# Narrow tiles paired in one PSUM bank, and the stream's steps forwarded by 400 instructions, in an attention with interleaved feed-forward work

## The chip, the cores and the metric

The kernel runs on one core of a Trainium2 chip: TensorE (matmuls, into PSUM), VectorE, ScalarE, GpSimd, and the queue of SyncE, which issues all DMAs here. The metric is the device time of one execution in microseconds. Rows of the profile call the engines PE (PEld: its weight loads), DVE, ACT, POOL and SP.

## What is computed

Three stages in a row, in float32, on B = 2 batches, 8 heads, 768 positions of head dimension 64; after the attention that is 1536 tokens of width 512:

```python
scores = scale * np.matmul(q, k.transpose(0, 1, 3, 2))
keep = is_sink | in_window            # 4 sink columns, window of 128
a = softmax(np.where(keep, scores, -1e9))
x = np.matmul(a, v)                   # -> 1536 x 512
h = x @ w_in                          # 512 -> 2048
x = (h * np.tanh(log1p(exp(h)))) @ w_out     # 2048 -> 512
p = domain_probs / domain_probs.sum(-1)      # 4 experts
out = sum(p[:, e] * (np.maximum(x @ w1[e], 0) @ w2[e]) for e in range(4))   # 512 -> 1024 -> 512
```

## The kernel before

**Attention.** `banded` walks 24 items (batch, block of 256 queries, pair of heads; the pairs run fastest, so that four items in a row finish 256 tokens). An item makes four score tiles on TensorE (L231), a masked copy with row minimum on VectorE (L234), the exponential on ScalarE (L238), a scaling on GpSimd (L252, L255), transposes (L264), and the product with the values, one tile `pv` of matmuls L277 and L283. `evac_x` then copies `pv` into the token matrix as a high part `xh` (ScalarE, L184) and a low part `xl` (VectorE, L185). There is one `pv` buffer, so the next item's `pv` waits for this copy. Items 0 to 23 are counted below; L185 of an item is called its evacuation.

**Feed-forward.** It is cut into units of 512 hidden columns: four units with the smooth activation, then eight of the experts. A product is done as three matmuls of high and low parts (`TERMS`). `stream` takes one chunk of tokens of a unit after the other: `layer1` makes hidden tiles `h` of 128 hidden columns by the chunk's tokens (L477), `mish` turns each into `gh` and `gl` (five ScalarE passes and the copy `gh`, VectorE L553, L555 and L556, GpSimd for `gl`), and `layer2` makes output tiles `o` (L504) and copies them into `acc`. Unit 0 is cut into chunks of 256, 256, 512 and 512 tokens, called c0 to c3. Chunk c0 needs items 0 to 3, c1 items 4 to 7, c2 items 8 to 15, c3 items 16 to 23. Each tile is a step of the generator; layer 1 of a chunk and layer 2 of the one before alternate. The loop over the items takes a step at every item from 5 on.

During the attention `h` and `o` have one PSUM bank each, and `mish` one buffer `r`; a new `h` waits until L556 has read the one before. When the attention's pools close, three banks each and two for `r` take their place (`x.psum(ctx, 3, 3, 2)`), and the weights of unit 1 (`wi1`, `wo1`) are loaded into memory that the attention's pools and that `r` held.

**Weights.** The first two layers' weights come as 64-bit numbers. `split_double` converts a quarter of a matrix at a time by seven VectorE passes over 1024 columns (L117 to L124). Ten such conversions lie within the attention: four for unit 0, six for `wi1`, `wo1` and `wi2`, which are parked in DRAM and loaded later. The eleventh, for `wo` of unit 2, is put out later in the program.

**Order.** The program is handed to a list scheduler. Each instruction has a place in the order in which the code puts it out; by its own timeline the scheduler picks, for each engine, among the instructions that are ready the one with the earliest place. The engines then run their lists in that order, each waiting where its next instruction is not ready. All DMAs stand in SP's one list.

## Time and profile before

| | us |
|---|---|
| runs shown | 929.54, 937.5, 939.44 (median 937.5) |
| the profiled execution, its own time | 931.33 |
| its span, first to last instruction | 929.5 |
| TensorE busy | 905.6 |
| VectorE, ScalarE, GpSimd busy | 424.6, 347.7, 263.7 |

The span holds all but 1.8 us of the profiled time. "Busy" of TensorE joins pipelined matmuls with modelled ends, so it is no measure of how full the engine is. The first 164 us hold the attention, the rest the feed-forward stages.

### The profile page before, as it was taken

To read this page: it belongs to the slowest core of one execution; us is meant where nothing else is said; L and a number is where in the kernel's file an instruction comes from. 1 tells how busy PE (TensorE), PEld (TensorE's weight loads), DVE (VectorE), ACT (ScalarE), POOL (GpSimd) and SP (SyncE) were. 2 spreads that over 40 slices of the span, in tenths; PEclk is the share of its full clock that TensorE was granted. 3 is DMA by queue.
4 is the path that set the end of the run, shared out by engine and by line. 5 is a ranking of instruction groups with operands and counts; after the bars stand their busy time and mean duration, and the time that the engine had idled before them with its cause. 6 is when DMAs were issued, how large, how long until landed. Compare 5 with 4: busy or idle time off the path is not lost.

```text
span 929.5 us, 11138 instructions
## 1 busy us (share of the span) xinstructions
PE 905.6 (97%) x4292; PEld 730.6 (79%) x4292; DVE 424.6 (46%) x770; ACT 347.7 (37%) x745; POOL 263.7 (28%) x217
## 2 busy tenths in 40 slices
PE   6999999799999999999999999999999999999997
PEld 4566767688888888888888888888888888888886
DVE  6999995247698555641112222222222222222222
ACT  4788875487767767722221111111111111111110
POOL 4586663122222434520220220221122112200000
PEclk8999999989999999999999999999999999999999
DMA  7757752062123011001110110110110010000012
GB/s 234 249 189 242 251 215 80 17 255 91 46 90 136 1 46 46 23 23 46 46 40 7 45 46 1 46 46 0 46 46 24 23 45 1 1 1 1 11 46 83
DMA packets 33790, 67.03 MB, mean 72 GB/s; under 512 B 4144, under 2 KB 12592, under 8 KB 33728
## 3 DMA queue, kind: packets, MB, share of 16 engines
q1 hardware_dynamic: 33728, 66.23, 21.1%
q8 instruction: 36, 0.59, 0.3%
q14 instruction: 26, 0.21, 0.1%
HBM read 51.54 MB, written 9.44 MB: 66 GB/s over the span
## 4 chain that ended last, share of the span: by engine, by line
PE 86%; DVE 10%; ACT 1%; DMA 1%; issue 0%; POOL 0%; DVEq 0%; ACTq 0%
PE h L477 42%; PE o L528 28%; PE o L504 14%; DVE pr L234 2%; DVE cv_h L119 1%; DVE cv_a L123 1%; PE pv L277 1%; DVE cv_a L117 1%; DVE cv_r L122 1%; DMA stage<-in_moe_w_in_dram 1%; PE sc L231 1%; PE tp L264 1%; DVE cv_a L121 1%; DVE xl L185 1%; DVE cv_a L118 0%
## 5 line engine op out<-in xcount | busy, mean ns | idle before, releaser
L477 PE MATMUL h<-xh,wih 128*128 128x512 f32 (+1 forms) x592 | 229.2, 387 | 0.3 <-DVE w L556 0.3
L477 PE MATMUL h<-xh,wil 128*128 128x512 f32 (+1 forms) x592 | 227.8, 385 | 0.0
L477 PE MATMUL h<-xl,wih 128*128 128x512 f32 (+1 forms) x592 | 226.8, 385 | 0.0
L486 ACT ACTIVATE gh<-h 128x512 fp32r<-128x512 f32 x96 | 57.4, 598 | 410.1 <-PE h L477 245.2
L487 DVE SCALAR_TENSOR_TENSOR gl<-h,gh 128x512 fp32r<-128x512 f32 x96 | 66.4, 691 | 208.1 <-ACT gh L486 207.9
L528 PE MATMUL o<-wol,gh 128*128 128x512 f32 (+1 forms) x388 | 150.1, 387 | 0.0
L528 PE MATMUL o<-woh,gh 128*128 128x512 f32 (+1 forms) x388 | 150.1, 387 | 0.0
L528 PE MATMUL o<-woh,gl 128*128 128x512 f32 (+1 forms) x388 | 149.9, 387 | 0.0
L536 DVE SCALAR_TENSOR_TENSOR acc<-o,pn,acc 128x512 f32<-128x512 f32 (+1 forms) x85 | 63.3, 745 | 176.2 <-PE o L528 176.2
L477 PEld LDWEIGHTS h<-xh,wih 128*128 128x128 f32 x592 | 111.8, 189 | 24.5 <-DVE cv_a L117 0.7
L477 PEld LDWEIGHTS h<-xl,wih 128*128 128x128 f32 x592 | 111.5, 189 | 22.6 <-issue 0.5
L477 PEld LDWEIGHTS h<-xh,wil 128*128 128x128 f32 x592 | 111.7, 189 | 22.3 <-DVE wil L124 0.3
L97 POOL TENSOR_TENSOR gl<-w,gh 128x512 fp32r<-128x512 f32 (+1 forms) x52 | 68.2, 1312 | 168.0 <-ACT gh L89 167.8
L504 PE MATMUL o<-gh,woh 128*128 128x512 f32 (+1 forms) x208 | 79.4, 382 | 5.4 <-ACT gh L89 5.4
L528 PEld LDWEIGHTS o<-wol,gh 128*128 128x128 f32 x388 | 72.9, 188 | 14.9
L528 PEld LDWEIGHTS o<-woh,gh 128*128 128x128 f32 x388 | 72.9, 188 | 14.9
L528 PEld LDWEIGHTS o<-woh,gl 128*128 128x128 f32 x388 | 72.8, 188 | 14.7
L504 PE MATMUL o<-gh,wol 128*128 128x512 f32 (+1 forms) x208 | 78.2, 376 | 0.0
L504 PE MATMUL o<-gl,woh 128*128 128x512 f32 (+1 forms) x208 | 77.4, 379 | 0.0
L87 POOL TENSOR_SCALAR wih<-stage 128x1024 fp32r<-128x1024 f32 x16 | 16.5, 1048 | 189.4 <-PE h L477 189.4
L553 DVE SCALAR_TENSOR_TENSOR u<-w,r 128x512 f32<-128x512 f32 (+1 forms) x52 | 34.4, 662 | 50.2 <-ACT r L552 49.9
L87 POOL TENSOR_SCALAR woh<-stage 128x1024 fp32r<-128x1024 f32 x16 | 16.5, 1048 | 141.0 <-PE o L528 122.2
(84 smaller groups left out, 1101.5 us busy)
## 6 DMA issues: line engine op xcount, KB each, us to landing
stage<-in_moe_w_dram SPq DMA_DIRECT2D x32, 512.0 KB, 3.7
stage<-in_moe_w_in_dram SPq DMA_DIRECT2D x8, 1024.0 KB, 6.6
stage<-in_moe_w_out_dram SPq DMA_DIRECT2D x8, 1024.0 KB, 5.0
qk<-in_qk_dram SPq DMA_DIRECT2D x16, 324.0 KB, 5.4
acc<-in_v_dram SPq DMA_DIRECT2D x16, 192.0 KB, 3.6
woh<-cv_h SPq DMA_DIRECT2D x6, 512.0 KB, 2.9
out_dram<-acc SPq DMA_DIRECT2D x11, 256.0 KB, 2.0
wih<-cv_h SPq DMA_DIRECT2D x4, 512.0 KB, 3.0
```

What stands on the lines that cost most here:

```text
L87: eng.tensor_scalar(out, src, 1.0, 0.0, ALU.mult, ALU.add)
L97: eng_lo.tensor_tensor(lo, src, hi.bitcast(F32), ALU.subtract)
L117: nc.vector.tensor_scalar(af, af, TINY_HI, HUGE_HI, ALU.max, ALU.min)
L119: nc.vector.scalar_tensor_tensor(h, w_hi, -0x40000000, a, ALU.bitwise_and, ALU.bitwise_or)
L234: nc.vector.tensor_tensor_reduce(out=o, in0=sc, in1=c.masks[t if i == 0 else 2][:, 0:sw], scale=-c.scale, scalar=3.0e38, op0=ALU.add, op1= ...
L477: nc.tensor.matmul(h, lhsT=wis[sw][:, k, fs], rhs=x[sx][:, k, cols], start=k == 0 and t == 0, stop=k == KT - 1 and t == 2,)
L486: nc.scalar.activation(gh, h, AF.Relu)
L487: nc.vector.scalar_tensor_tensor(gl, h, 0.0, gh.bitcast(F32), ALU.max, ALU.subtract)
L504: nc.tensor.matmul(o, lhsT=wos[sw][:, f, ds], rhs=g[f][sx], start=f == 0 and t == 0, stop=f == NF - 1 and t == 2,)
L528: nc.tensor.matmul(o, lhsT=g[f][sx][:, ds], rhs=wos[sw][:, f, ms], start=f == 0 and t == 0, stop=f == NF - 1 and t == 2,)
L536: nc.vector.scalar_tensor_tensor(y, o, pcol, y, ALU.mult, ALU.add)
L553: nc.vector.scalar_tensor_tensor(u, w, 1.0, r, ALU.add, ALU.mult)
```

## The change

`layer1` and `layer2` take as many tiles as fit into a bank of 512 columns: for the chunks of 256 tokens two hidden tiles stand side by side in one `h`, and two output tiles in one `o`, each pair with one set of passes behind it; a step is then a pair. Chunks of 512 are as before. Unit 0's four chunks have 20 steps in place of 28. They are taken at items 5, 7, 9, 11, 13, 15 and 17 to 23 (13 steps, in place of 19 at items 5 to 23), within `tc.high_priority(offset=FORWARD)`: the instructions of such a step get a place in the order that is 400 earlier (an item is some 40 instructions). Item 23's step is now the first `h` of c3, in the attention's bank; before it was an `o` of c1.

```diff
--- before.py
+++ after.py
@@ -26,8 +26,9 @@
 QW = 2 * P
 STAGE = 1024
 AHEAD = 2
-LAG = 5
 WARM = 12
+STEPS = (5, 7, 9, 11, 13, 15, *range(17, 24))
+FORWARD = 400
 PARK = (8, 10, 12, 14, 16, 18)
 
 class Ctx:
@@ -469,23 +470,26 @@
         x = (c.xh, c.xl)
         cols = slice(t0, t0 + cw)
         wis = self.w[n][0]
-        for f in range(NF):
-            h = self.pa.tile([P, self.CW], F32, tag="h", name="h")[:, 0:cw]
-            fs = slice(f * P, (f + 1) * P)
-            for k in range(KT):
-                for t, (sw, sx) in enumerate(TERMS):
-                    nc.tensor.matmul(
-                        h, lhsT=wis[sw][:, k, fs], rhs=x[sx][:, k, cols],
-                        start=k == 0 and t == 0, stop=k == KT - 1 and t == 2,
-                    )
-            gh = self.gp.tile([P, self.CW], F32R, tag="gh", name="gh")[:, 0:cw]
-            gl = self.gp.tile([P, self.CW], F32R, tag="gl", name="gl")[:, 0:cw]
+        m = self.CW // cw
+        parts = [slice(q * cw, (q + 1) * cw) for q in range(m)]
+        for f0 in range(0, NF, m):
+            h = self.pa.tile([P, self.CW], F32, tag="h", name="h")
+            for f, at in enumerate(parts, f0):
+                fs = slice(f * P, (f + 1) * P)
+                for k in range(KT):
+                    for t, (sw, sx) in enumerate(TERMS):
+                        nc.tensor.matmul(
+                            h[:, at], lhsT=wis[sw][:, k, fs], rhs=x[sx][:, k, cols],
+                            start=k == 0 and t == 0, stop=k == KT - 1 and t == 2,
+                        )
+            gh = self.gp.tile([P, self.CW], F32R, tag="gh", name="gh")
+            gl = self.gp.tile([P, self.CW], F32R, tag="gl", name="gl")
             if kind == 0:
                 self.mish(n, gh, gl, h)
             else:
                 nc.scalar.activation(gh, h, AF.Relu)
                 nc.vector.scalar_tensor_tensor(gl, h, 0.0, gh.bitcast(F32), ALU.max, ALU.subtract)
-            g.append((gh, gl))
+            g.extend((gh[:, at], gl[:, at]) for at in parts)
             yield
 
     def layer2(self, n, t0, cw, g):
@@ -496,22 +500,25 @@
         wos = self.w[n][1]
         if kind == 0:
             accv = self.acc.rearrange("p (ch d) w -> p ch d w", d=KT)
-            for d in range(KT):
-                o = self.pb.tile([P, cw], F32, tag="o", name="o")
-                ds = slice(d * P, (d + 1) * P)
-                for f in range(NF):
-                    for t, (sw, sx) in enumerate(TERMS):
-                        nc.tensor.matmul(
-                            o, lhsT=wos[sw][:, f, ds], rhs=g[f][sx],
-                            start=f == 0 and t == 0, stop=f == NF - 1 and t == 2,
-                        )
-                y = accv[:, t0 // c.DM, d, t0 % c.DM:t0 % c.DM + cw]
+            m = self.CW // cw
+            for d0 in range(0, KT, m):
+                o = self.pb.tile([P, self.CW], F32, tag="o", name="o").rearrange("p (m w) -> p m w", m=m)
+                for d in range(d0, d0 + m):
+                    ds = slice(d * P, (d + 1) * P)
+                    for f in range(NF):
+                        for t, (sw, sx) in enumerate(TERMS):
+                            nc.tensor.matmul(
+                                o[:, d - d0], lhsT=wos[sw][:, f, ds], rhs=g[f][sx],
+                                start=f == 0 and t == 0, stop=f == NF - 1 and t == 2,
+                            )
+                ds = slice(d0, d0 + m)
+                y = accv[:, t0 // c.DM, ds, t0 % c.DM:t0 % c.DM + cw]
                 if n == 0:
                     nc.scalar.activation(y, o, AF.Copy)
                 else:
                     nc.vector.tensor_tensor(y, y, o, ALU.add)
                 if n == n1 - 1:
-                    split(c, c.xh[:, d, cols], c.xl[:, d, cols], y, nc.scalar, nc.vector)
+                    split(c, c.xh[:, ds, cols], c.xl[:, ds, cols], y, nc.scalar, nc.vector)
                 yield
             return
         last = n == len(self.units) - 1
@@ -589,15 +596,16 @@
         attention_item(c, a, *it, preps.pop(m))
         if m < 4 or m in PARK:
             run(w, 1)
-        if m >= LAG:
-            run(steps, 1)
+        if m in STEPS:
+            with tc.high_priority(offset=FORWARD):
+                run(steps, 1)
         if m == 0:
             normalize_probs(c)
     first.close()
     x.wpool[1] = ctx.enter_context(tc.tile_pool(name="m_w1", bufs=1))
     x.psum(ctx, 3, 3, 2)
     run(x.weights(1))
-    run(steps, 4 * (x.NF + 4) - 4 - (len(items) - LAG))
+    run(steps, 2 + 4 + 6 + 8 - len(STEPS))
     rest(c, x, steps, 1)
```

Three places show what the scheduler made of it. Names carry buffer numbers; line numbers of the changed kernel are one higher in the attention, L481 for L477 and L510 for L504.

VectorE at the evacuation of item 19 (`pv_1709` before, `pv_1641` now); the rows named `cv` are the eleventh conversion. First the kernel before, then the changed one.

```order
L234 ISA pr_1969,mx_1970<-sc_1980,mask260_90 128x260
L234 ISA mx_1970 128x1
L185 TENSOR_TENSOR xl_95<-pv_1709,xh_94 128x256
L234 ISA pr_1969,mx_1970<-sc_1984,mask260_90 128x260
L234 ISA mx_1970 128x1
L555 SCALAR_TENSOR_TENSOR u_1321<-u_1321,r_1322 128x256
L556 SCALAR_TENSOR_TENSOR w_1320<-u_1321,h_1305 128x256
L117 TENSOR_SCALAR cv_a_2400<-cv_a_2400 128x1024
L118 TENSOR_SCALAR cv_a_2400<-cv_a_2400 128x1024
L240 RECIPROCAL sm_1971<-sm_1971 128x4
L119 SCALAR_TENSOR_TENSOR cv_h_2402<-stage_60,cv_a_2400 128x1024
L185 TENSOR_TENSOR xl_95<-pv_1779,xh_94 128x256
```

```order
L118 TENSOR_SCALAR cv_a_2328<-cv_a_2328 128x1024
L119 TENSOR_SCALAR cv_a_2328<-cv_a_2328 128x1024
L120 SCALAR_TENSOR_TENSOR cv_h_2330<-stage_60,cv_a_2328 128x1024
L241 RECIPROCAL sm_1846<-sm_1846 128x4
L122 TENSOR_SCALAR cv_a_2328<-cv_h_2330 128x1024
L123 TENSOR_SCALAR cv_r_2329<-cv_h_2330 128x1024
L235 ISA pr_1925,mx_1926<-sc_1936,mask260_90 128x260
L235 ISA mx_1926 128x1
L124 SCALAR_TENSOR_TENSOR cv_a_2328<-stage_60,cv_a_2328 128x1024
L235 ISA pr_1925,mx_1926<-sc_1940,mask260_90 128x260
L235 ISA mx_1926 128x1
L186 TENSOR_TENSOR xl_95<-pv_1641,xh_94 128x256
```

Six passes of the eleventh conversion stood behind that evacuation and stand ahead of it now.

TensorE after the last hidden tile that uses the attention's bank: `h_1941`, the fourth of c2, before; `h_1978`, the first of c3, now. `gh_1803` and `gh_1910` belong to the tile before it in that bank, `gh_1954` to `h_1941`, and `gh_1991` to `h_1978`. First before, then changed.

```order
L477 MATMUL h_1941<-xl_95,wih_227 128x512
L504 MATMUL o_2139<-gh_1803,woh_353 128x512
L504 MATMUL o_2139<-gh_1803,wol_354 128x512
L504 MATMUL o_2181<-gh_1803,woh_353 128x512
L504 MATMUL o_2181<-gh_1803,wol_354 128x512
L504 MATMUL o_2223<-gh_1803,woh_353 128x512
L504 MATMUL o_2223<-gh_1803,wol_354 128x512
L504 MATMUL o_2139<-gl_1804,woh_353 128x512
L504 MATMUL o_2181<-gl_1804,woh_353 128x512
L504 MATMUL o_2223<-gl_1804,woh_353 128x512
L504 MATMUL o_2139<-gh_1954,woh_353 128x512
L504 MATMUL o_2139<-gh_1954,wol_354 128x512
```

```order
L481 MATMUL h_1978<-xl_95,wih_227 128x512
L510 MATMUL o_2067<-gh_1910,woh_353 128x512
L510 MATMUL o_2067<-gh_1910,wol_354 128x512
L510 MATMUL o_2067<-gl_1911,woh_353 128x512
L510 MATMUL o_2109<-gh_1910,woh_353 128x512
L510 MATMUL o_2109<-gh_1910,wol_354 128x512
L510 MATMUL o_2109<-gl_1911,woh_353 128x512
L510 MATMUL o_2151<-gl_1483,woh_353 128x512
L510 MATMUL o_2151<-gh_1581,woh_353 128x512
L510 MATMUL o_2151<-gh_1581,wol_354 128x512
L510 MATMUL o_2151<-gl_1582,woh_353 128x512
L510 MATMUL o_2151<-gh_1747,woh_353 128x512
```

Before, nine matmuls stand between the tile and the first use of its `gh`; in the changed kernel 28 do (the list goes on with `o_2151` and `o_2165`, then `o_2239<-gh_1991`).

SP's queue at the end of the attention: `wi1`, `wo1` are unit 1's weights, `wi2` unit 2's first, which overwrites unit 0's. First before, then changed.

```order
L372 DMA stage_60<-in_moe_w_in_dram 128x2x1024
L434 DMA wih_2057<-wi1h_792 128x1024
L434 DMA wil_2058<-wi1l_793 128x1024
L434 DMA wih_2057<-wi1h_792 128x1024
L434 DMA wil_2058<-wi1l_793 128x1024
L434 DMA woh_2063<-wo1h_1137 128x1024
L434 DMA wol_2064<-wo1l_1138 128x1024
L434 DMA woh_2063<-wo1h_1137 128x1024
L434 DMA wol_2064<-wo1l_1138 128x1024
L434 DMA wil_2308<-wi2l_1451 128x1024
L434 DMA wih_2307<-wi2h_1450 128x1024 x2
```

```order
L373 DMA stage_60<-in_moe_w_in_dram 128x2x1024
L435 DMA wil_2236<-wi2l_1397 128x1024
L435 DMA wih_2235<-wi2h_1396 128x1024 x2
L435 DMA wil_2236<-wi2l_1397 128x1024
L435 DMA wih_2027<-wi1h_788 128x1024
L435 DMA wil_2028<-wi1l_789 128x1024
L435 DMA wih_2027<-wi1h_788 128x1024
L435 DMA wil_2028<-wi1l_789 128x1024
L435 DMA woh_2033<-wo1h_1115 128x1024
L435 DMA wol_2034<-wo1l_1116 128x1024
L435 DMA woh_2033<-wo1h_1115 128x1024
```

The four loads of `wi2` stood behind those of `wi1` and `wo1`, and stand ahead of them now.

## Rows read from the trace of the kernel before

**Rows 1.** The page: busy us (share) xcount; 40 slices in tenths; granted clock.

```profile
PE 905.6 (97%) x4292; PEld 730.6 (79%) x4292; DVE 424.6 (46%) x770; ACT 347.7 (37%) x745; POOL 263.7 (28%) x217
...
DVE  6999995247698555641112222222222222222222
...
PEclk8999999989999999999999999999999999999999
```

**Rows 2.** Four stretches: busy us (instructions) of each engine, granted clock, DMA share, GB/s.

```profile
100.00:120.00 20.00, 20.00 (x139) 14.47 (x140) 19.66 (x48) 17.23 (x54) 13.39 (x15) 1.00 0.82 280
120.00:140.00 20.00, 18.66 (x124) 12.62 (x125) 19.97 (x51) 15.72 (x48) 13.30 (x15) 0.91 0.54 193
140.00:160.00 20.00, 20.00 (x133) 16.18 (x130) 10.26 (x13) 11.05 (x28) 6.51 (x7) 1.00 0.23 81
180.00:200.00 20.00, 15.22 (x54) 12.29 (x55) 8.26 (x12) 15.10 (x28) 4.96 (x4) 0.83 0.77 284
```

**Rows 3.** Timeline of VectorE: start us, length us, what ran, [idle before].

```profile
138.20 0.41 DVE L185 TENSOR_TENSOR xl<-pv,xh 128x256 fp32r<-128x256 f32 x1
...
139.84 1.03 DVE L117 TENSOR_SCALAR cv_a<-cv_a 128x1024 f32<-128x1024 f32 x1
...
146.44 1.22 DVE L123 SCALAR_TENSOR_TENSOR cv_a<-stage,cv_a 128x1024 f32<-128x1024 uint32 x1
...
163.86 0.42 DVE L185 TENSOR_TENSOR xl<-pv,xh 128x256 fp32r<-128x256 f32 x1 [0.33 <-ACT xh L184]
```

**Rows 4.** VectorE groups by shape, 20 to 164 us: xcount | busy, mean ns.

```profile
L555 DVE SCALAR_TENSOR_TENSOR u<-u,r 128x256 f32<-128x256 f32 x8 | 3.5, 434 | 0.0
...
L555 DVE SCALAR_TENSOR_TENSOR u<-u,r 128x512 f32<-128x512 f32 x2 | 1.4, 692 | 1.4 <-ACT u L554 1.4
```

**Rows 5.** Timeline of TensorE in the attention.

```profile
128.49 0.38 PE L477 MATMUL h<-xh,wih 128*128 128x256 f32 x1 [0.25 <-DVE w L556]
...
161.68 1.09 PE L277 MATMUL pv<-pt,acc 128*64 128x256 f32 x12
...
163.34 0.96 PE L477 MATMUL h<-xl,wih 128*128 128x512 f32 x3
```

**Rows 6.** The chain that ended last, steady stage: start us, us, what.

```profile
421.24 2.72 PE h L477 x12
```

**Rows 7.** Timeline of TensorE after the attention.

```profile
177.00 0.39 PE L477 MATMUL h<-xl,wih 128*128 128x512 f32 x1
...
178.59 0.84 PE L504 MATMUL o<-gl,woh 128*128 128x512 f32 x3
184.78 0.79 PE L504 MATMUL o<-gh,woh 128*128 128x512 f32 x1 [5.35 <-ACT gh L89]
...
191.19 0.40 PE L477 MATMUL h<-xh,wih 128*128 128x512 f32 x1
```

**Rows 8.** Timelines of ScalarE and, last two, VectorE in the same stretch.

```profile
177.49 1.09 ACT L549 ACTIVATE w<-h 128x512 f32<-128x512 f32 x2 [2.49 <-PE h L477]
...
184.10 0.63 ACT L89 ACTIVATE gh<-w 128x512 fp32r<-128x512 f32 x1 [1.55 <-DVE w L556]
...
188.31 0.58 ACT L510 ACTIVATE acc<-o 128x512 f32<-128x512 f32 x1
...
182.58 0.69 DVE L555 SCALAR_TENSOR_TENSOR u<-u,r 128x512 f32<-128x512 f32 x1 [0.69 <-ACT u L554]
183.38 0.69 DVE L556 SCALAR_TENSOR_TENSOR w<-u,h 128x512 f32<-128x512 f32 x1
```

**Rows 9.** SP: one issue; then groups of loads, KB each, us to landing.

```profile
183.42 0.34 SPq L434 DMA_DIRECT2D wih<-wi1h  x1
...
wih<-wi1h SPq DMA_DIRECT2D x2, 512.0 KB, 5.6
...
wih<-wi2h SPq DMA_DIRECT2D x2, 512.0 KB, 8.6
```

## The prediction

> **What bounds the kernel now.** I read the slices first: TensorE's clock is full nearly throughout and VectorE is at nine tenths only in the first seventh of the span [rows 1]. Behind 200 us twelve matmuls of 512 columns take 2.72 us [rows 6], or 0.227 us each, without a gap; what the change leaves of that stage is the same list of matmuls, so it can be gained only that TensorE has fewer of them left when the attention ends, or loses less time there. So I read the stretches of the attention. From 100 to 140 us VectorE is busy 39.6 of 40 us [rows 2]: it is the bound. TensorE reads as full too, with 20.00 of 20, but its weight loads take 14.47 and 12.62 us of 20 there against 16.18 in the next stretch [rows 2], where VectorE is half idle and TensorE works down what it has. So TensorE has room while VectorE is the bound.
>
> The Trainium skill says the same way of reading (Perfetto Trace Analysis, Identifying the Most-Contended Engine): matmul busy time is no measure of how full TensorE is, the share of its weight loads is a better one. Were the busy row right instead, work moved forward would push the attention back by its whole length; that is the second rival below.
>
> The evacuation of item 19 starts at 138.20 us and that of item 23 at 163.86 [rows 3]. Then comes the hand-over to the wide stage: the last hidden tile of the single bank ends at 177.2 us (177.00 and 0.227), nine matmuls follow, and TensorE stands idle for 5.35 us until that tile's `gh` comes [rows 7]. After it the granted clock is at the lower level, until about 191 [rows 7]; 0.83 over 180 to 200 us [rows 2] is 3.4 us of lost work. The hand-over loses 5.35 + 3.4 = 8.75 us.
>
> **Pairing.** The eight narrow tiles of c0 and c1 become four. A pass of 256 columns takes 0.434 us on VectorE, one of 512 0.692 [rows 4]: a pair saves 0.18 us a pass, three passes and four pairs 2.1 us. That goes where VectorE is the bound. ScalarE saves passes too, but it isn't full there (17.23 and 15.72 of 20 [rows 2]), so I take nothing for it. Against that, a second-half matmul can no longer run while the first half is worked on. In this kernel it couldn't before either: with one bank, a narrow tile started when VectorE had read the tile before, after 0.25 us of idling [rows 5]. A pair takes 2.84 us on TensorE where a single took 1.42 (24 and 12 halves of 0.118, estimated as half of 0.227 and a little), and this lengthens the chain of tiles by no more than it saves in four runs through the passes.
>
> The Trainium skill advises the opposite (Perfetto Trace Analysis, Matmuls): independent groups should rotate through different banks, so that one is evacuated while the next is computed. By that rule four pairs would lose 4 x 1.42 = 5.7 us of overlap. Row 128.49 shows that there was none to lose [rows 5], so I leave it out of the sum.
>
> **What forwarding moves on TensorE.** I counted the matmuls of L477 and L504 in the two orders, in units of 512 columns. Ahead of the `pv` of item 12 stand 75 in place of 35.5, of item 19 120 in place of 76.5, of item 23 168 in place of 138. At the end of the attention 30 more are done: 30 x 0.227 = 6.8 us that need not be done later. That is the gain, if the attention ends at the same time.
>
> **When the attention ends.** VectorE's list ahead of item 19's evacuation now holds six passes of the eleventh conversion, which stood behind it. In the trace these run from 139.84 to 147.66 us, less an evacuation and a small operation between them, some 7.3 us [rows 3]. The hidden tiles' passes there cost alike: eight narrow tiles begun and seven ended before, five wide ones now. Since VectorE was full until then, the evacuation slips; I take 6.8 us, as its records overlap a little: 145.0 us. From item 19's evacuation to item 23's it was 25.7 us [rows 3], and TensorE set it: 61.5 matmuls x 0.227 = 13.9 us, four `pv` of 1.66 us each (161.68 to 163.34 [rows 5]) = 6.6 us, and 5.1 us of transposes and scores. Now 48 matmuls are left, 10.9 us, and the rest is the same: 22.6 us, less about 1.3 us of transposes that TensorE can do while it waits for the evacuation. So item 23's evacuation comes at 145.0 + 22.6 - 1.3 = 166.3 us, 2.4 us later than before. The bounds: 1 us earlier than before, if the conversion's passes fill time in which VectorE would have waited for scores; 12 us later, if all of the moved matmuls delay the scores as well (second rival). I take 2.4 because the VectorE list up to item 21 is equally long in both orders, so VectorE itself ends the attention no later.
>
> **The hand-over.** The last tile of the old bank is now the first of c3. Its `gh` took 7.5 us from the last matmul before (177.2 to 184.73 [rows 7, 8]). In ScalarE's new list three copies of `o` stand between its passes, of about 0.55 us each by the row at 188.31 [rows 8]: 9.2 us. TensorE has 28 matmuls in hand for that time in place of nine, 6.35 us; it idles about 2.85 us in place of 5.35. I leave the lower clock after it at 3.4 us. Then unit 1's first `h` needs `wi1`. Its load still waits for L555 of the last tile in `r`, whose end (183.27) is the time of the issue, 183.42 [rows 8, 9], and it now stands behind the four loads of `wi2`. Those wait only for that tile's matmuls, about 8 us sooner, and take 8.6 us to land, so they are through when `wi1` is issued; `wi1` takes 5.6 [rows 9]. By then TensorE, slowed by the clock, has used up the first nine matmuls of c3's outputs; I put 1 us for what it waits, with 0 to 6 as bounds. The hand-over then loses 2.85 + 3.4 + 1 = 7.25 us, 1.5 less than before. The steady stage behind it has the same work and, as before, weights in time; I put nothing for it.
>
> **The sum.** +2.4 - 6.8 - 1.5 = -5.9 us. On the profiled execution's 931.33 us this is 925.4. That execution is 6 us below the median of the runs shown, 937.5; the four executions average 934.45, and I set the prediction on this: 934.45 - 5.9 = **928.5 us**. A measurement of this kernel tells about 1% from no change.
>
> **Rivals.** *No idling at the hand-over.* If 28 matmuls cover the activation and `wi1` lands in time, the clock stays up as well: +2.4 - 6.8 - 8.75 = -13.2 us, 921 us. For it speaks that the scheduler put the 28 there; against it the chain of 9.2 us.
>
> *Slower: the blocks delay the scores.* Each pair is a block of up to 24 matmuls, 2.84 us, in front of scores in TensorE's list, and there are three score banks for VectorE to live on. If VectorE starves as long as the extra matmuls take until item 19 (43.5 x 0.227 = 9.9 us) and has the conversion to do as well, item 23's evacuation comes 12.3 us late: +12.3 - 6.8 - 1.5 = +4, 938.5 us. It decides from a slip of 8.3 us, where the gain is used up. Against it: VectorE had conversions to fill such gaps and was never idle from 100 to 140 us [rows 2].
>
> *The load queue.* If the loads of `wi2` are still in flight when `wi1` is issued, the two share the bandwidth and `wi1` lands up to 8.6 us later. TensorE then idles 6 us more at the lower clock: -5.9 + 6 = 0, 934.5 us.
>
> That the change does nothing of what it says I can exclude: the orders differ as told.
>
> **How the numbers follow.** The forecast has 0.60, no idling 0.13, the blocks 0.13, the load queue 0.14. Around each I allow some 4 us, since three runs of the kernel before lie 10 us apart. More than 1% under the median of 937.5 is below 928.1: nearly half of the forecast's cases, nine tenths of the first rival's and little else, 0.41. Slower by over 1%, above 946.9, is left to the tails of the last two and what I don't see, 0.07. Within 1%: 0.52. The range is 919 to 939: it leaves out the best of the first rival and the worst of the second.
>
> **What would show it.** In the new profile: more matmuls of L481 and L510 before 140 us; VectorE still full there, with the evacuation of item 19 at about 145 us and of item 23 at 165 to 168; one idle stretch of TensorE at about 180 us of 3 us in place of 5.35, ended by `gh` again; `wi2`'s loads issued ahead of `wi1`'s. Wrong would be: VectorE idle for scores before 140 us (the blocks), TensorE idle for a load at 185 to 195 us (the queue), no idling there (the first rival), or new gaps behind 200 us, for which I have no case.

## The result: slower by 1.2%, and where the time went

The changed kernel took 946.77 us (median of four executions, 946.35 to 949.39) against 936.25 for the kernel before on the same chip (929.54 to 939.44): a ratio of 1.0123, 95% interval 1.0082 to 1.0163. The prediction was 928.5, with a range up to 939: wrong in direction and outside the range. The profiled execution took 946.82 us, its span 945.0. One execution of a later kernel, `late`, is left out as slow (970.36 us, mean clock 0.935).

I compared the two traces by a count. Take every matmul of L477 and L504 (L481 and L510 now; for N = 3300 also those of the experts' second layer, L528 and L535) in the order in which TensorE runs them, two of 256 columns as one, and note when the N-th starts:

| N | before, us | after, us | difference |
|---|---|---|---|
| 100 | 149.3 | 121.5 | -27.8 |
| 138 | 161.4 | 167.3 | +5.9 |
| 200 | 177.5 | 187.9 | +10.4 |
| 230 | 192.8 | 194.7 | +1.9 |
| 260 | 199.6 | 207.0 | +7.4 |
| 500 | 254.0 | 263.8 | +9.7 |
| 700 | 299.4 | 314.9 | +15.5 |
| 3300 | 888.7 | 904.2 | +15.5 |

At 122 us the changed kernel is 28 us ahead on this work; by the end of the attention that is gone. It catches up at the hand-over (N = 200 to 230), loses that again behind it, and loses 8.1 us more from N = 260 to 700. Then nothing changes. Some 4 us of the 15.5 are chance, told below, which leaves about 11, the difference of the medians.

**The page and the four stretches of the changed kernel**, as in [rows 1, 2]:

```profile
PE 918.0 (97%) x4292; PEld 734.9 (78%) x4292; DVE 428.9 (45%) x758; ACT 345.4 (37%) x717; POOL 263.3 (28%) x213
...
DVE  6899987236779544762112222222223222222222
...
PEclk8799997999999999999999999999999999999999
```

```profile
100.00:120.00 20.00, 18.83 (x119) 12.20 (x118) 19.59 (x55) 15.05 (x45) 12.90 (x13) 1.00 0.72 229
120.00:140.00 20.00, 18.70 (x123) 12.61 (x123) 17.69 (x44) 16.21 (x48) 10.46 (x13) 1.00 0.77 271
140.00:160.00 20.00, 19.37 (x87) 12.51 (x85) 15.53 (x36) 12.34 (x35) 12.58 (x14) 0.66 0.26 91
180.00:200.00 20.00, 17.48 (x81) 14.08 (x77) 4.57 (x7) 9.19 (x18) 1.39 (x2) 0.99 0.33 111
```

VectorE was full from 100 to 140 us before; now it is busy 17.69 of 20 from 120 to 140. The granted clock from 140 to 160 us is 0.66, where before it was 1.00.

**VectorE in the attention**: its waits for scores, before (20 to 164 us) and now (20 to 182 us; line waited for: us in all, times, longest), and three rows of its timeline, to be held against [rows 3]:

```profile
DVE pr L234 <- PE sc L231: 0.3, 1, 0.3
```

```profile
DVE pr L235 <- PE sc L232: 8.4, 10, 2.5
```

```profile
158.28 0.43 DVE L235 CUSTOM_DVE_ANT_0 pr<-sc,mask 128x260 f32<-128x260 f32 x1 [2.53 <-PE sc L232]
...
160.12 0.42 DVE L186 TENSOR_TENSOR xl<-pv,xh 128x256 fp32r<-128x256 f32 x1
...
181.26 0.42 DVE L186 TENSOR_TENSOR xl<-pv,xh 128x256 fp32r<-128x256 f32 x1
```

The evacuation of item 19 starts at 160.12 us (138.20 before), that of item 23 at 181.26 (163.86). VectorE, the engine that I took for the bound, waits 8.4 us for TensorE's scores, where it waited 0.3.

**TensorE in the middle and at the hand-over**: two pieces of the chain that ended last, then rows of the timeline, against [rows 5 to 7]:

```profile
151.24 4.71 PE h L481 x12
...
420.44 2.72 PE h L481 x12
```

```profile
143.26 1.97 PE L278 MATMUL pv<-pt,acc 128*64 128x256 f32 x12
...
190.62 0.39 PE L481 MATMUL h<-xl,wih 128*128 128x512 f32 x1
...
199.87 0.80 PE L510 MATMUL o<-gh,woh 128*128 128x512 f32 x1 [2.52 <-ACT gh L90]
...
204.71 0.50 PE L481 MATMUL h<-xh,wil 128*128 128x512 f32 x1 [0.77 <-DMA wil<-wi1l]
```

Twelve matmuls that take 2.72 us later took 4.71 at 151 us; a `pv` group of 1.09 us [rows 5] took 1.97. The trace's clock rows give the lower level (1.2 GHz) from 141.7 to 155.3 us. At the hand-over TensorE idles 2.52 us for `gh` and 0.77 for `wi1`.

**The hand-over on ScalarE, then SP** (issues, then groups of loads with us to landing), against [rows 8, 9]:

```profile
191.11 1.09 ACT L556 ACTIVATE w<-h 128x512 f32<-128x512 f32 x2 [7.06 <-PE h L481]
...
199.19 0.63 ACT L90 ACTIVATE gh<-w 128x512 fp32r<-128x512 f32 x1 [1.07 <-DVE w L563]
```

```profile
190.81 0.34 SPq L435 DMA_DIRECT2D wil<-wi2l  x1
...
198.43 0.32 SPq L435 DMA_DIRECT2D wih<-wi1h  x1
...
wih<-wi2h SPq DMA_DIRECT2D x2, 512.0 KB, 5.9
wih<-wi1h SPq DMA_DIRECT2D x2, 512.0 KB, 6.7
```

`gh` came 9.0 us after the last matmul of the tile (190.85 to 199.82). `wi2` is issued ahead of `wi1`, as in the new order, and costs under 1 us.

**New gaps in the wide stage.** The stretch from 230 to 312 us in the kernel before, which shows no wait of TensorE, and TensorE's waits there in the changed kernel:

```profile
230.00:312.00 82.00, 82.00 (x363) 67.92 (x362) 66.70 (x90) 56.95 (x97) 22.71 (x16) 1.00 0.23 86
```

```profile
PE h L481 <- DVE w L563: 5.3, 6, 1.4
```

With one wait of 0.6 us for a copy of `o`, TensorE reads as idle for 5.8 of the 8.1 us; the other 2.3 go with the restart after the seven gaps.

One of them, on VectorE and then TensorE:

```profile
298.38 0.68 DVE L118 TENSOR_SCALAR cv_a<-cv_a 128x1024 f32<-128x1024 f32 x1
...
300.81 2.20 DVE L120 SCALAR_TENSOR_TENSOR cv_h<-stage,cv_a 128x1024 int32<-128x1024 int32 x1
...
305.39 0.68 DVE L560 SCALAR_TENSOR_TENSOR u<-w,r 128x512 f32<-128x512 f32 x1
305.99 1.22 DVE L125 SCALAR_TENSOR_TENSOR wol<-cv_a,cv_r 128x1024 fp32r<-128x1024 f32 x1
...
308.50 0.69 DVE L563 SCALAR_TENSOR_TENSOR w<-u,h 128x512 f32<-128x512 f32 x1
```

```profile
309.25 0.50 PE L481 MATMUL h<-xh,wih 128*128 128x512 f32 x1 [1.39 <-DVE w L563]
```

Six passes of a conversion stand in VectorE's list ahead of a tile's first pass, from 298.38 to 305.39 us, and the seventh behind it. L563 frees that tile's bank only at 309.2, and the next matmul in TensorE's list waits for it.

### The profile page after: what moved, and what is told of

It reads as the page before. It is cut to its first block, busy times and chain, and to the rows that moved or that the text cites. A ratio compares the mean times of both kernels' runs of the same rounds, so it can differ in the third digit from the quotient of the medians.

```text
span 945.0 us, 11100 instructions
## 1 busy us (share of the span) xinstructions
PE 918.0 (97%) x4292; PEld 734.9 (78%) x4292; DVE 428.9 (45%) x758; ACT 345.4 (37%) x717; POOL 263.3 (28%) x213
## 4 chain that ended last, share of the span: by engine, by line
PE 81%; DVE 10%; issue 3%; ACT 2%; DMA 2%; POOL 1%; SPq 0%; DVEq 0%; POOLq 0%; ACTq 0%
PE h L481 38%; PE o L535 28%; PE o L510 9%; PE sc L232 2%; PE pv L278 2%; PE tp L265 1%; DVE pr L235 1%; DVE cv_h L120 1%; DVE u L562 1%; DVE cv_a L124 1%; DVE cv_a L122 1%; DVE cv_a L118 1%; DVE u L560 1%; DMA stage<-in_moe_w_in_dram 1%; DMA wil<-wi1l 1%
## 5 line engine op out<-in xcount | busy, mean ns | idle before, releaser
L481 PE MATMUL h<-xh,wih 128*128 128x512 f32 (+1 forms) x592 | 231.0, 390 | 5.3 <-DVE w L563 5.3
L481 PE MATMUL h<-xh,wil 128*128 128x512 f32 (+1 forms) x592 | 228.8, 386 | 0.8 <-DMA wil<-wi1l 0.8
L481 PE MATMUL h<-xl,wih 128*128 128x512 f32 (+1 forms) x592 | 228.4, 387 | 0.0
L535 PE MATMUL o<-wol,gh 128*128 128x512 f32 (+1 forms) x388 | 150.1, 387 | 0.0
L535 PE MATMUL o<-woh,gh 128*128 128x512 f32 (+1 forms) x388 | 150.1, 387 | 0.0
L535 PE MATMUL o<-woh,gl 128*128 128x512 f32 (+1 forms) x388 | 149.9, 387 | 0.0
L481 PEld LDWEIGHTS h<-xh,wih 128*128 128x128 f32 x592 | 112.6, 190 | 31.7 <-DVE w L563 8.0
L481 PEld LDWEIGHTS h<-xl,wih 128*128 128x128 f32 x592 | 112.0, 190 | 23.7 <-issue 0.7
L481 PEld LDWEIGHTS h<-xh,wil 128*128 128x128 f32 x592 | 112.5, 190 | 23.0 <-DMA wil<-wi1l 1.2
L98 POOL TENSOR_TENSOR gl<-w,gh 128x512 fp32r<-128x512 f32 x48 | 66.7, 1391 | 171.9 <-ACT gh L90 166.4
L535 PEld LDWEIGHTS o<-wol,gh 128*128 128x128 f32 x388 | 72.9, 188 | 15.0
L535 PEld LDWEIGHTS o<-woh,gl 128*128 128x128 f32 x388 | 72.9, 188 | 14.8
L535 PEld LDWEIGHTS o<-woh,gh 128*128 128x128 f32 x388 | 72.8, 188 | 14.7
L510 PE MATMUL o<-gh,woh 128*128 128x512 f32 (+1 forms) x208 | 79.1, 380 | 3.1 <-ACT gh L90 2.5
L510 PE MATMUL o<-gh,wol 128*128 128x512 f32 (+1 forms) x208 | 77.9, 376 | 0.0
L510 PE MATMUL o<-gl,woh 128*128 128x512 f32 (+1 forms) x208 | 73.0, 376 | 0.0
L560 DVE SCALAR_TENSOR_TENSOR u<-w,r 128x512 f32<-128x512 f32 x48 | 34.0, 710 | 61.8 <-ACT r L559 61.8
```

The source lines that it names most:

```text
L98: eng_lo.tensor_tensor(lo, src, hi.bitcast(F32), ALU.subtract)
L481: nc.tensor.matmul(h[:, at], lhsT=wis[sw][:, k, fs], rhs=x[sx][:, k, cols], start=k == 0 and t == 0, stop=k == KT - 1 and t == 2,)
L510: nc.tensor.matmul(o[:, d - d0], lhsT=wos[sw][:, f, ds], rhs=g[f][sx], start=f == 0 and t == 0, stop=f == NF - 1 and t == 2,)
L535: nc.tensor.matmul(o, lhsT=g[f][sx][:, ds], rhs=wos[sw][:, f, ms], start=f == 0 and t == 0, stop=f == NF - 1 and t == 2,)
L560: nc.vector.scalar_tensor_tensor(u, w, 1.0, r, ALU.add, ALU.mult)
```

## The experiments

Three theories stood after the result. **A, the attention:** matmuls put ahead of scores delay the attention by their length, because TensorE has no room in it. **B, the eleventh conversion:** its passes, now ahead of item 19's evacuation, hold VectorE up; this was my prediction's reason for a slip. **C, the wide stage:** the order of conversions behind the attention makes gaps there, whatever the attention does. All ratios are to the kernel before on the same chip, with 95% intervals. "Low" is time of TensorE at its lower clock level in the profiled execution.

**One half of the change alone.** `pair_only` is the changed kernel without the forwarding:

```diff
-            with tc.high_priority(offset=FORWARD):
-                run(steps, 1)
+            run(steps, 1)
```

> The narrow tiles paired and the steps at the items of the changed kernel, without the forwarding. In the two orders the matmuls of unit 0 ahead of item 19's pv are 120 with and without it, so if the pairing costs the time (a denser stream in the stretch where VectorE is the bound), this runs at 943 to 949 us and item 23's evacuation comes at 176 to 183 us, as in the changed kernel. If the forwarding costs it (blocks of matmuls put in front of the scores), it runs at 926 to 935 us and item 23's evacuation comes at 163 to 167.

`forward_only` is the kernel before with the forwarding, every tile single:

```diff
+FORWARD = 400
...
-            run(steps, 1)
+            with tc.high_priority(offset=FORWARD):
+                run(steps, 1)
```

> The narrow tiles as before, with the steps at items 5 to 23 forwarded by 400. If the pairing costs the time: 930 to 940 us, as before, with item 23's evacuation within 2 us of 164. If the forwarding does: 942 us or more, with VectorE waiting several us for scores, which it did for 0.3 us before.

Measured: 946.19 us, 1.0111 [1.0054, 1.0169], and 946.57 us, 1.0113 [1.0039, 1.0187]. Either half costs as much as both, but not in the same way. In the orders, 75, 120 and 171 matmuls stand ahead of the `pv` of items 12, 19 and 23 with pairing alone, 36, 76.5 and 138 with forwarding alone: it is the pairing that moves the work, since a narrow tile no longer waits for the passes of the one before. I had put that down to the forwarding. With forwarding alone item 23's evacuation is 11.1 us late (174.97) all the same, with no matmul more ahead of it: 17.1 us more of low since item 3 make 8.5, and VectorE waits 6.9 us for scores. The forwarding also alters the scheduler's list behind the attention. With it alone TensorE's waits from 180 to 330 us are these:

```profile
PE o L505 <- ACT gh L90: 5.4, 1, 5.4
PE h L478 <- DVE w L557: 3.3, 1, 3.3
```

The first is the hand-over of before; the second is new, ends at 308 us, and the clock is low for 6.8 us from 306.9 on. From N = 600 to 700 this run loses 6.3 us.

**Conversions left out.** `noconv_after` and `noconv_before` load unit 1's parked weights in place of converting those of units 2 and 3, so the conversions from the eleventh on are not computed and the output is another. The edit is the same in both:

```diff
-            if (n, nm) in self.parked:
+            if (n, nm) in self.parked or (self.parked and n in (2, 3)):
...
-                    for t, d in zip((hi, lo), self.parked[n, nm]):
+                    for t, d in zip((hi, lo), self.parked[(n, nm) if (n, nm) in self.parked else (1, nm)]):
```

> The changed kernel with unit 1's converted weights loaded in place of converting wo of unit 2 and both matrices of unit 3, so that it leaves out the conversions of the eleventh on. If the new gaps of TensorE from 207 to 312 us (8 us more behind at matmul 700 than at 260) are tiles whose passes wait behind conversions in VectorE's list, they are gone here: the time falls by 6 to 9 us beside the changed kernel, to some 938. If they come from the order in which the stream's own steps stand, they stay and the time is 944 or more. The eleventh conversion is also gone ahead of item 19's evacuation: if it is what VectorE had too much, that evacuation comes 5 to 7 us sooner than in the changed kernel, at about 154 us.

> The kernel before with the same conversions left out. It had no gaps there, so by either theory its time moves by less than 4 us (929 to 938), and what noconv_after is behind it is what the attention and the hand-over cost: 7 to 9 us by the first theory, 13 to 16 by the second.

Measured: 940.08 us, 1.0043 [1.0014, 1.0073], and 933.94 us, 0.9977 [0.9947, 1.0007]. Evacuations of items 19 and 23 in `noconv_after`, and its stretch from 230 to 312 us:

```profile
158.70 0.42 DVE L186 TENSOR_TENSOR xl<-pv,xh 128x256 fp32r<-128x256 f32 x1
...
177.96 0.42 DVE L186 TENSOR_TENSOR xl<-pv,xh 128x256 fp32r<-128x256 f32 x1 [3.18 <-ACT xh L185]
```

```profile
230.00:312.00 82.00, 82.00 (x363) 67.91 (x362) 41.68 (x64) 57.83 (x99) 21.68 (x17) 1.00 0.21 72
```

B falls: without the eleventh conversion item 19's evacuation comes only 1.4 us sooner (158.70 against 160.12). C holds: there is no gap left between N = 260 and 700. The 6.1 us between the two kernels' medians are about what the change costs without the gaps. It is not a clean difference, since other things moved too: from N = 200 to 260 `noconv_after` loses 8.9 us where the changed kernel loses 5.5.

`noconv_before` had low for 20.5 us from 15 us on, where the profiled execution of the kernel before had 6.8, though both run the same list there. Item 3's evacuation comes 3.3 us late and its N = 100 to 200 come 3.5 to 4.1 us late, and in all it is +2.5 us. That is the chance part of the changed kernel's 15.5 us: it too had 20.5.

**No stream in the attention.** `late` is the changed kernel with all steps behind the attention:

```diff
-STEPS = (5, 7, 9, 11, 13, 15, *range(17, 24))
+STEPS = ()
...
-            with tc.high_priority(offset=FORWARD):
-                run(steps, 1)
+            run(steps, 1)
```

> The changed kernel with no step of the stream inside the attention; all 20 follow it, unforwarded. It gives the length of the attention alone. If the stream's matmuls are free in the attention (they fill time in which TensorE waits for VectorE), the evacuation of item 19 comes only by the stream's passes on VectorE sooner than before: 7 tiles x 0.87 us = 6 us, at 132 us in place of 138.6, and item 23's at about 140, since it has 127 matmuls x 0.227 = 29 us less to fit in from item 19 on. If they delay the scores one for one, 76.5 x 0.227 = 17 us more goes ahead of item 19: at 115 us. After it 127 matmuls more stand than in the kernel before, 29 us; the time is 940 to 955 by the first, 925 to 935 by the second. The waits of VectorE for scores (L235 on L232) should then be near nothing by both.

Measured: 951.9 us, 1.0185 [1.0136, 1.0234]. The time lies in the range of the first case, but neither case describes the attention: item 19's evacuation came at 144.30 us, 6 us later than before, with 76.5 matmuls fewer ahead of it, and VectorE's waits for scores are the longest of all these runs. Two stretches, and VectorE's waits for scores up to 163 us:

```profile
80.00:100.00 20.00, 19.26 (x77) 12.42 (x76) 13.18 (x43) 9.53 (x31) 9.92 (x10) 0.54 0.54 169
...
120.00:140.00 20.00, 20.00 (x108) 12.29 (x107) 13.59 (x41) 11.78 (x38) 11.81 (x13) 0.77 0.56 196
```

```profile
DVE pr L235 <- PE sc L232: 14.9, 13, 4.0
```

The granted clock is 0.54 from 80 to 100 us, where the attention's own matmuls are all that TensorE has; in this run it is low for 41.9 us between the evacuations of items 3 and 19, against 5.6 before. Half of the difference, 18.1 us, is about what 76.5 matmuls fewer would have saved (17.4), and item 3 itself came 5.5 us late. TensorE looks full at that level and VectorE waits for it. So taking the stream out of the attention gave nothing back, because the clock was lower there; that was in neither of my two cases. That the stream's matmuls hold the clock up is a guess from this: `late` had the full clock from 47 to 81 us without any, and no run changes the clock alone.

**Fewer pairs, later.** `pair_late` has steps at eight items, not forwarded:

```diff
-STEPS = (5, 7, 9, 11, 13, 15, *range(17, 24))
+STEPS = (12,15,18,19,20,21,22,23)
```

> The changed kernel without the forwarding and with steps at items 12, 15 and 18 to 23 alone: paired tiles, but 72, 84 and 144 matmuls ahead of the pv of items 12, 19 and 23 in place of 75, 120 and 168 (35.5, 76.5 and 138 in the kernel before), and in the list of VectorE behind the attention the conversions stand as in the kernel before (at most four passes in a row) in place of up to seven. Theory: blocks of matmuls ahead of scores delay the attention, and the order of conversions makes the gaps behind it. Then up to item 13 it is as late as the changed kernel (+8), no further slip to item 19 (147 to 150 us), item 23 about 172, no gaps of the steady stage: +8 - 1.4 for six more matmuls = +6 or so, 942. Rival: what costs is the pairing itself (passes of a pair, no overlap within a bank), whatever stands where: then 945 to 947 again. Rival: lower clock alone makes the middle slip, and it comes here as well.

Measured: 941.19 us, 1.0069 [1.0033, 1.0105]. The median is as theories A and C have it, but the attention is not: item 23's evacuation was at 189.44 us (172 expected), with the clock low for 30.7 us from 136.5 on, where 12 matmuls stand between the `pv` of items 13 and 19. There are no gaps behind it and no idling at the hand-over. The profiled execution was one of the two longest of nine (947.15 us, mean clock 0.966; the shortest 936.13, 0.984). Over the whole span, 0.018 of clock is some 34 us of low, more than the early stretches of all profiles differ by (6.8 to 23.9), so the clock in the middle probably varies from execution to execution, and the time with it; no trace of a short one is there to show it.

**One layer paired.** `pair_o` pairs the outputs, `pair_h` the hidden tiles. Each takes `layer1` or `layer2` of the changed kernel into the kernel before, with 24 steps in all; the diff is that of `pair_o`, and `pair_h` has `STEPS = (5, 7, *range(9, 24))`:

```diff
-LAG = 5
+STEPS = (*range(5, 21), 23)
...
-        if m >= LAG:
+        if m in STEPS:
...
-    run(steps, 4 * (x.NF + 4) - 4 - (len(items) - LAG))
+    run(steps, 24 - len(STEPS))
```

> The kernel before with only the output tiles of c0 and c1 paired, the hidden tiles single, 17 steps at items 5 to 20 and 23, not forwarded. Its order has as many stream matmuls ahead of the pv of items 12 and 19 as the kernel before (35.5 and 76.5), 159 in place of 138 ahead of item 23, and behind the attention the same order of conversions as the changed kernel (runs of six and seven passes). Theory: the attention ends about as before (evacuation of item 19 at 139, of 23 at 166 to 170), 21 matmuls x 0.227 = 4.8 us are gained there, and the steady stage loses 6 to 8 us in gaps after hidden tiles waiting for L556: +2 to +6 us in all, 938 to 942. Rival: the gaps come from a late start of the stage rather than from the order of the conversions: then none here, 930 to 934.

> The kernel before with only the hidden tiles of c0 and c1 paired, the output tiles single, 17 steps at items 5, 7 and 9 to 23, not forwarded. Its order has 75, 120 and 171 stream matmuls ahead of the pv of items 12, 19 and 23, as with both layers paired, and the changed kernel's order of conversions behind the attention. Theory: the hidden tiles alone bring the lateness, so it is like the kernel with both paired: evacuation of item 19 at 152 to 160, of item 23 at 178 to 182, gaps of 6 to 8 us behind it, 944 to 947. Rival: the outputs' pairs matter as much; then half of it, 940.

Measured: 954.29 us, 1.0228 [1.0182, 1.0275], and 943.12 us, 1.0101 [1.0057, 1.0145]. `pair_h` is near what was expected (944 to 947). `pair_o` is 12 us worse than I had thought, but not in the wide stage. There it waits as the changed kernel does:

```profile
PE h L477 <- DVE w L559: 5.3, 6, 1.4
PE o L506 <- DVE acc L515: 0.6, 1, 0.6
```

These are its waits from 230 to 322 us, and the first is the changed kernel's to the tenth, with another attention ahead. From item 23's evacuation on VectorE's list is the same, row by row, in the traces of the changed kernel, `pair_only` and `pair_h` (388 rows), and in `pair_o` but for four near its start; all four lose 8.1 us from N = 260 to 700. `late` and `pair_late`, with another list, lose none. The rest of `pair_o`'s excess is in the attention (the early low, and 3.5 us more idling of TensorE between items 13 and 19) and at the hand-over, where from N = 200 to 260 it loses 4.4 us more than the kernel before.

**TensorE's room, measured.** `twice` is the kernel before with each hidden tile of c0 and c1 computed twice into the same place:

```diff
-            for k in range(KT):
-                for t, (sw, sx) in enumerate(TERMS):
-                    nc.tensor.matmul(
+            for _ in range(2 if cw < self.CW else 1):
+                for k in range(KT):
+                    for t, (sw, sx) in enumerate(TERMS):
+                        nc.tensor.matmul(
```

> The kernel before with the matmuls of every hidden tile of c0 and c1 done twice, the second set over the first: 48 matmuls of 512 columns more in the attention (36 of them ahead of item 13's pv, 46 ahead of item 19's), with no other work moved but by the scheduler's new order, which behind the attention is like that of the forwarded kernel before (about 6 us of gaps there). Theory, new: TensorE is full in the attention as well, so whatever goes ahead costs its length: item 13's evacuation 36 x 0.227 = 8 us later, item 19's 10.6 us later (149 us, and up to 4 more where the early half-clock stretch is long), item 23's 11 us; the time 935 + 10.9 + 6 = 952. Rival, the prediction's: TensorE has room while VectorE is the bound: item 19's evacuation at 139 to 143 us, item 23's 2 to 5 us later, the time about 941.

Measured: 950.22 us, 1.0141 [1.0101, 1.0181], or 13.2 us more by the ratio and 14.0 between the medians. The 48 matmuls make 10.9, a new gap of 1.5 us behind the attention with the restart after it 1.8. The evacuations of items 13, 19 and 23:

```profile
118.86 0.41 DVE L185 TENSOR_TENSOR xl<-pv,xh 128x256 fp32r<-128x256 f32 x1
...
157.43 0.42 DVE L185 TENSOR_TENSOR xl<-pv,xh 128x256 fp32r<-128x256 f32 x1
...
183.33 0.42 DVE L185 TENSOR_TENSOR xl<-pv,xh 128x256 fp32r<-128x256 f32 x1 [1.63 <-ACT xh L184]
```

Item 19's is 19.2 us late, where the rival had 1 to 5: 46.5 x 0.227 = 10.6 by the matmuls, 3.8 by the early low, 2.3 by more low behind it (10.2 us against 5.6) and 2.9 by more idling of TensorE between items 3 and 19 (7.3 us against 4.4), 19.6 in all. Work added to TensorE while VectorE read as full [rows 2] cost its whole length, so TensorE had no room. This is theory A.

**One step less.** `after_12` is the changed kernel without the step at item 23, so that the first `h` of c3 no longer uses the attention's bank:

```diff
-STEPS = (5, 7, 9, 11, 13, 15, *range(17, 24))
+STEPS = (5, 7, 9, 11, 13, 15, *range(17, 23))
```

> The changed kernel with 12 steps in the attention in place of 13: the first hidden tile of c3 is no longer in the attention's bank. In the attention the order is the same up to item 23 (120 and 168 matmuls ahead of the pv of items 19 and 23). Behind it the last tile in the old bank has 42 matmuls or more behind it before its gh is used, in place of 28, and VectorE's list has the conversions as in the kernel before. Theory: of what the change costs, 8 us are the gaps made by the order of conversions behind the attention, 3 to 5 the hand-over; the attention's slip stays (evacuation of item 19 about 160 us, of 23 about 180). So N-th matmul 700 against 300 shows no loss and the time is 947 - 8 - 3 = 934 to 938. Rival: the loss of the steady stage follows from the late end of the attention: then 943 to 947.

Measured: 932.63 us, 0.9967 [0.9942, 0.9992], 14 us less than the changed kernel, a little less than the kernel before and 1.4 below what was expected. The attention is the same (evacuations of items 19 and 23 at 159.29 and 180.44 us). What differs stands behind it; the changed kernel's stretch first, then that of `after_12` and its hand-over:

```profile
230.00:312.00 82.00, 76.16 (x328) 60.57 (x327) 68.91 (x88) 53.11 (x87) 21.49 (x15) 1.00 0.27 97
```

```profile
230.00:312.00 82.00, 82.00 (x364) 67.89 (x363) 67.42 (x90) 56.61 (x95) 21.59 (x15) 1.00 0.24 89
...
180.00:200.00 20.00, 20.00 (x88) 16.54 (x89) 9.58 (x15) 16.73 (x30) 5.07 (x4) 1.00 0.79 279
```

In the same 82 us TensorE did 36 matmuls more, 36 x 0.227 = 8.2 us. And it went through the hand-over at the full clock, without idling: from the end of item 23's evacuation to N = 260, 92 matmuls, it took 19.8 us in place of 25.3. The sum is 13.7 of the 14.

**Two versions by the same reasoning.** `before_12` is the kernel before with 12 steps, `pair_even` the paired kernel without forwarding and with ten:

```diff
-LAG = 5
+STEPS = range(5, 17)
```

```diff
-STEPS = (5, 7, 9, 11, 13, 15, *range(17, 24))
+STEPS = (5, 8, 11, 14, 17, 18, 19, 20, 21, 22)
```

> The kernel before with 12 steps in the attention (items 5 to 16) in place of 19. Its order is that of before up to item 15; 72 and 128 matmuls stand ahead of the pv of items 19 and 23 in place of 76.5 and 138, and 64 or more behind the last tile of the old bank before its gh is used, in place of 10. Theory: work that is not done in the attention costs its length later and the same in the attention, so it is neutral; what counts are idle and half-clock stretches of TensorE. The hand-over loses nothing in place of 5.35 + 3.4 us: 935 - 8.7 = 926, unless TensorE, with fewer matmuls at items 17 to 20, falls to the lower clock there (as without any stream: up to 5 us back). Rival: TensorE has room in the attention: then 10 matmuls fewer there cost 2.3 us and the gain is 6: 929. Both beat the two kernels.

> The changed kernel without the forwarding, with 10 steps at items 5, 8, 11, 14 and 17 to 22: 75, 108 and 150 matmuls ahead of the pv of items 12, 19 and 23, the conversions behind the attention in the order of the kernel before, and 53 matmuls or more of cushion at the hand-over. Theory: no steady gaps, no idling at the hand-over, about 8 us less than the kernel with both layers paired for the one and 3 for the other: 934 to 937, like the kernel before; stretches at half clock in the attention, if long, add half of their length. Rival: the pairing itself costs (longer passes, a bank that is busy longer): 943 to 947.

Measured: 929.86 us, 0.9944 [0.9909, 0.9979], and 937.82 us, 1.0015 [0.9992, 1.0037]. `before_12` beats both kernels by the same means as `after_12`:

```profile
180.00:200.00 20.00, 20.00 (x93) 16.66 (x92) 7.26 (x11) 15.73 (x29) 5.17 (x4) 1.00 0.38 135
```

TensorE is busy throughout where it had 15.22 of 20 at a clock of 0.83 before [rows 2]. Of the 8.6 us that the hand-over cost, 10.2 us of low at 144 us, in place of 3.4 at 136, take 3.4 back: 5.2 us, and by the ratio it gains 5.2. It does not tell the two cases of its expectation apart (926, with up to 5 us back by the clock, and 929). `pair_even` came out 0.8 us above what was expected (934 to 937), and well below the 943 of its rival, that pairing itself costs.

## Why the prediction was wrong

**The account that holds.** For each profiled run I took the time up to N = 700, less TensorE's idle time, less half of its time at the lower clock:

| run | to N = 700, us | idle | low | rest |
|---|---|---|---|---|
| before | 299.4 | 19.0 | 20.4 | 270.2 |
| noconv_before | 301.9 | 16.4 | 37.5 | 266.8 |
| before_12 | 301.4 | 15.7 | 30.7 | 270.3 |
| after_12 | 300.4 | 13.0 | 34.1 | 270.3 |
| pair_even | 305.6 | 16.3 | 30.7 | 274.0 |
| after | 314.9 | 22.1 | 41.0 | 272.2 |
| noconv_after | 309.6 | 18.4 | 41.0 | 270.7 |
| pair_only | 313.9 | 23.1 | 27.3 | 277.1 |
| pair_h | 310.5 | 21.3 | 23.9 | 277.2 |
| forward_only | 316.3 | 23.8 | 44.3 | 270.3 |
| pair_o | 321.8 | 29.3 | 40.9 | 272.0 |
| pair_late | 315.2 | 14.9 | 64.8 | 267.9 |
| late | 320.1 | 18.3 | 71.7 | 265.9 |

`twice` is counted to N = 748, for its 48 matmuls more: 318.8 us, 19.5 idle, 41.0 low, a rest of 278.8, or 267.9 without the 10.9 us of those matmuls. The rest is 266 to 274 us in 11 of the 13 others; it is least where low is longest (`late`, `pair_late`), so half is a little too high a price for low. This is what one sees where TensorE bounds the attention as well as what follows, and a matmul costs about the same wherever it stands. Then moving work gains nothing by itself; what counts are TensorE's idle stretches and those at the lower clock. In `pair_only` and `pair_h` the rest is 277; what takes those 7 us I did not settle.

**What bounds the kernel: the step that failed.** "So TensorE has room while VectorE is the bound" is false. The busy row, 20.00 of 20 [rows 2], was right, and I set it aside for the weight loads' share, by the rule of the Trainium skill that I cited (Perfetto Trace Analysis, Identifying the Most-Contended Engine). That share was 14.47 and 12.62 of 20 in stretches where added matmuls cost their full length. For this stage the measurement goes against the rule's second half, the share; the first measure that it names, MFU, I did not work out. What I wrote ahead of the prediction, that the busy row is no measure of how full TensorE is, misled me in the same way here. I had written down what would follow, as the second rival.

**When the attention ends.** Predicted +2.4 us, measured +17.4 at item 23's evacuation. Of it 4.0 are there at item 3's already, by the early low. Of the other 13.4, the 30 matmuls more make 6.8, the clock 5.1 (between items 3 and 23 it was low for 17.1 us against 6.8, half of the difference) and TensorE's idling 1.4 (5.8 us against 4.4): 13.3. The clock inside the attention was no term of my sum. The work of the stream had run out: in the new order 108 matmuls stand ahead of the `pv` of item 16, 17 and 18 alike, and there the clock fell. The eleventh conversion, for which I had put 6.8 us of slip, had next to no part in it: 1.4 us by `noconv_after`.

**What forwarding moves.** 30 matmuls more were done by item 23, as counted; but the pairing did it, and the -6.8 us were paid for in the attention.

**The hand-over** went as predicted in kind and nearly in size: 2.52 us of idling for `gh` (2.85), 0.77 for `wi1` (1), but 1.7 us by the clock (3.4) since it was low for 3.4 us only. With some 0.5 us of start-up it lost 5.5 from N = 200 to 260, where the kernel before lost 8.6: -3.0 us, where I had -1.5.

**The steady stage**, for which "I put nothing", lost 8.1 us. It is the largest term that I had at nothing, and I had no case for it; the sum without it would be +3.5 us, no change that can be told. I compared VectorE's order only up to item 21.

The sum with these sizes: 6.8 + 5.1 + 1.4 - 6.8 - 3.0 + 8.1 = 11.6 us. The two traces differ by 15.5 less the 4.0 of the early low, 11.5, the medians by 10.5.

**The second rival** had the mechanism of the attention, the starving of VectorE and a price near it (12.3 us late for 13.4), and gave 938.5. That the price is so near is partly luck: it was 9.9 us of matmuls up to item 19 and 2.4 by the conversion, where 6.8 of matmuls up to item 23, 5.1 of clock and 1.4 of idling were measured. With the wide stage's 8.1 it would have been 946.6.

**Pairing.** That a pair loses no overlap in the bank held as far as can be seen: no wait of a tile for its bank shows in the attention of the changed kernel (one of 1.4 us in `pair_even`), and `after_12`, paired throughout, is no slower than the kernel before. Whether pairing gains its 2.1 us can't be told: `after_12` and `before_12`, both without the hand-over and the gaps, have overlapping intervals.

**What stays open.** What takes the 7 us of `pair_only` and `pair_h`; why `forward_only`, with the stream's count of the kernel before, was at the lower clock for 17.1 us from 129 on, and which instructions keep the clock up. The runs with a drop in the middle mostly have few stream matmuls there, but no run changes the clock alone.

## What to carry to other kernels

Where a second stream of work is woven into a stage that is full on one engine, first find out whether the other engine has room by adding dummy work to it; a share of weight loads did not tell. If it has none, moving work sooner is neutral, and only what the new order does to idle stretches, buffers that change hands and the clock is worth pricing. With a list scheduler, compare the whole order of every engine, far behind the edit too: one step more or less here moved 14 us, 8 of them in a stage that the edit did not touch.

## What the runs showed of the hardware that was not expected

The half-clock stretch at the start of the attention (from 13 to 18 us on) was 6.8 us long in two profiled runs, 13.7 to 23.9 us in the other twelve, also where the list up to there is the same. Where 20.5 stood for 6.8, item 3's evacuation came 3.3 to 4.0 us later (`noconv_before`, the changed kernel). It is probably part of why executions of the kernel before lie 10 us apart: one of 930.12 us had a mean clock of 0.989, one of 939.29 had 0.979.

The attention's own matmuls do not always run at the upper clock: in `late`, with nothing else on TensorE, the clock was full from 47 to 81 us and at the lower level from 81 to 105, with TensorE busy for 19.26 of 20 from 80 to 100. An engine that reads as full is not always a fast one.

In some rows of the changed kernel VectorE and GpSimd held each other up, and the one that began second ran longer by about the overlap. The conversion's third pass (L120) took 1.22 us at 228.82, with GpSimd idle, and 2.20 at 300.81, where GpSimd was on the second of two `gl` until 301.92. At 275.09 it began 0.11 us ahead of a `gl` and took 1.23; the `gl` took 2.27. At 238.18 a `gl` began first and took 1.29; the pass L119, 0.16 us behind it, took 1.69, where it takes 0.68 at 274.38. No run tests it. The pass L562 took 0.90 us on average in the new attention, where the same pass took 0.69 before [rows 4]; why is open.
